# A fused retention and mixture-of-experts kernel: whole scores for the first eight tiles, earlier weights and tokens, and a new order of the first pass

## The chip, the cores and the metric

The kernel runs on one NeuronCore of a Trainium2 chip. The core has a matrix engine (TensorE; the profile calls its products PE and its weight loads PEld), VectorE (DVE), ScalarE (ACT), GpSimd (POOL) and SyncE (SP, which here only issues DMAs and reads registers). The metric is the device time of one execution in microseconds; lower is better.

## The reference, cut to what matters

The inputs are q, k, v (8 batches, 8 heads, 576 positions, 64 wide). Their retention output is the token matrix x (4608 x 512), and each token goes to one of 16 experts.

```
scores = q @ k.T / sqrt(64);  ret = scores * gamma[h] ** (i - j) for i >= j, else 0;  attn = ret @ v
x = attn, heads side by side                          # 4608 x 512
g = argmax(x @ w_group);  e = argmax(x @ w_expert[g]) # 4 groups of 4 experts
out[token] = g_w * e_w * (relu(x @ w1[g, e]) @ w2[g, e])   # 512 -> 1024 -> 512, g_w and e_w: softmax weights
```

## The kernel before

**Retention.** The tokens are cut into 36 tiles of 128 (t = 0 to 35; every ninth holds the last 64 positions of two batches). A loop over t works on several tiles at once. ACT scales the eight heads of v (`vs`, eight instructions, `scale(t + 1)`). TensorE multiplies the scaled values with the masked scores (`px`, `av(t - 1)`), adds to a running state (`pst`, `state(t)`), adds the part of the state (`px<-a,st`, `inter(t - 1)`) and makes the next scores (`pss`, `scores(t + 1)`). DVE scales the finished tile into `xT` (`turned(t - 1)`) and masks the new scores into `sT` (`masked(t + 1)`). There is one `px` buffer, so that the next `px` waits for `turned`. The scores leave out the blocks above the diagonal: 16 products of 64 x 64 weights and 128 or 64 columns per tile, on the four quarters of the array. Each f32 product leaves two PE records and two PEld records.

**Routing.** For each group of three tiles TensorE makes the logits (`plt`, then turned, `pl`), DVE picks the expert (`choose`: lg, mx, df, oh, ob), counts places (`pp`, `places`: pr, sl) and weighs (`weigh`: wt). TensorE turns each tile (`pxt`, `xnat_pe`), ACT writes it, weighted, to `xt` (`xnat_out`), and POOL writes token numbers beside it (iota) and scatters its rows into the DRAM buffer `xs`, sorted by expert (`xnat_store`).

**Experts.** 17 passes (p = 0 to 16) of eight steps f: `layer1(p, f)` makes `ph`, ACT takes relu to `hh`, `layer2(p, f)` adds to `py`. Weights come in four pieces a pass (`load_piece`, 2 x 512 KB, tiles `r`); they and the tokens are split into a high and a low part on ACT and DVE (`wh`, `wl`), except for the first six steps of pass 0 (`WHOLE`), which multiply in plain f32. Pass 0 handles the first 256 tokens of the fullest expert of the first tiles, which `pick(0)` finds while the retention still runs; `expert_of` reads its number into a register of SP, `xload(p)` loads the tokens (four DMAs, `xb<-xs`, for pass 0 256 rows of 2112 bytes), and `xturn` turns them on DVE. Pass 1 needs all tokens scattered. The last 128 columns of work (p = 16) end the kernel (`last1`: `phn`; `last_tr`: `pth`); one scatter of POOL each writes the results.

**Order.** After the set-up each engine runs its instructions in the order of the code (`Ordered`, `pin`), and all of them show as line L117, where the helper issues them. SP's loads, too, stay in the code's order: a load that waits holds up those behind it. The loads of tiles and of weights share two rings of seven buffers (`r1`, `r2`). The change touches the constants, `xnat_pe`, `xnat_out`, `xnat_store`, `layer1`, `scores`, the set-up loads, the retention loop from t = 31 (r = t - 26), the first two passes and the last.

Of the kernel before, what the change touches and what calls it, by code (L numbers as in the profile page):

```python
# [7 lines left out]
F32 = mybir.dt.float32  # L8
F32R = mybir.dt.float32r
# [19 lines left out]
WHOLE = 6  # L29
RB = 7  # L30
LOADS = 7
WARM = 32
NS = N + P
NT = N // P
NPIECE = 4
# [31 lines left out]
def moe_retention(ctx, tc, qk, kv, wgt, w1, w2, c_f, out):  # L67
# [92 lines left out]
    def load_piece(i):  # L160
        if i < len(pieces):
            raws[i] = wload(*pieces[i])
# [5 lines left out]
    def whole(p, f):  # L168

        return p == 0 and f < WHOLE  # L170
# [18 lines left out]
    def nblocks(p):  # L189
        return -(-CS[p] // 32)  # L190

    def natural(p):
        return p in (0, E)
# [136 lines left out]
    def xnat(t):  # L330
        xnat_pe(t)
        xnat_out(t)
        xnat_store(t)

    def xnat_pe(t):

        T = tiles[t]
        T["pxt"] = ps_tr.tile([P, NKC, P], F32, name=f"pxt_{t}", tag="tr")
        for i in range(NKC):
            pe.transpose(T["pxt"][:, i, :], T["xT"][:, i, :], ident)  # L340

    def xnat_out(t):
        T = tiles[t]
        g_ = tiles[T["grp"][-1]]
        r = t - T["grp"][0]
        pxt = T["pxt"]
        xt = T["xt"] = gp.tile([P, Q, WQ], F32, name=f"xt_{t}", tag="xt", bufs=3)
        act.activation(xt[:, :, 0:DQ], pxt, AF.Copy, scale=g_["wt"][:, r : r + 1])

    def xnat_store(t):  # L350
        T = tiles[t]
        g_ = tiles[T["grp"][-1]]
        r = t - T["grp"][0]
        xt = T["xt"]
        for b, s0, p0, n in T["rng"]:
            pool.iota(
                xt[p0 : p0 + n, :, DQ:WQ].bitcast(I32), pattern=[[1, Q], [0, WQ - DQ]],
                base=Q * (b * S + s0), channel_multiplier=Q,
            )
# [160 lines left out]
    def without():  # L520
        dve.tensor_scalar(mi0, sln, picked["c0"], float(BIG), ALU.is_ge, ALU.mult)

    obs = []
    wgp = gp.tile([P, NKC, 32], F32, name="wgp")


    with ExitStack() as ac:
# [70 lines left out]
        pw = ps_sm.tile([P, P], F32, name="pw", tag="sm")  # L598
# [26 lines left out]
        def scores(t):  # L625

            T = tiles[t]
            for i in range(0, NP, 2):  # L630
# [95 lines left out]
        for t in range(NT + 1):  # L726
# [60 lines left out]

# [60 lines left out]
    def layer1(p, f):  # L848
        i = p * NPIECE + f // 2
        C = CS[p]  # L850
        if (p, f) == (0, 0):
            ph = ps_st.tile([P, CMAX], F32, name=f"ph_{p}_{f}", tag="tr")
        elif p == 0:
            ph = psy.tile([P, CMAX], F32, name=f"ph_{p}_{f}", tag=f"py{f % 2}")
        else:
            pool_ = (ps_sm, ps_tr, ps_sm, ps_st)[f % 4]
            ph = pool_.tile([P, CMAX], F32, name=f"ph_{p}_{f}", tag="sm" if f % 2 == 0 else "tr")
        cs = slice((f % 2) * P, (f % 2) * P + P)
        hh = mp.tile([P, CMAX], F32R, name=f"hh_{p}_{f}", tag="hh", bufs=4)
        if whole(p, f):  # L860
            for kc in range(NKC):
                pe.matmul(
                    ph[:, :C], raws[i][0][:, kc, cs], xTf[p][:, kc, :C], start=kc == 0, stop=kc == NKC - 1
                )
            act.activation(hh[:, :C].bitcast(F32), ph[:, :C], AF.Relu)
            hts[p, f] = (hh.bitcast(F32), None)
            return
        wh, wl = wsp[i, 0]
        xh, xl = xTs[p]
        n = 0  # L870
        for kc in range(NKC):
            for a, b in ((wh, xh), (wh, xl), (wl, xh)):
                pe.matmul(
                    ph[:, :C], a[:, kc, cs], b[:, kc, :C], start=n == 0, stop=n == 3 * NKC - 1
                )
                n += 1
        C32 = 32 * nblocks(p)
        if f == 0 and C32 > C and not natural(p):

            dve.memset(hh[:, C:C32].bitcast(F32), 0.0)  # L880
        hl = mp.tile([P, CMAX], F32R, name=f"hl_{p}_{f}", tag="hl", bufs=4)
        act.activation(hh[:, :C], ph[:, :C], AF.Relu)
        dve.scalar_tensor_tensor(
            hl[:, :C], ph[:, :C], 0.0, hh[:, :C].bitcast(F32), ALU.max, ALU.subtract
        )
        hts[p, f] = (hh, hl)

    def layer2(p, f):
        if f == 0:
# [95 lines left out]
    for p in range(E):  # L985
        for f in range(NFC):
            pc = p * NPIECE + f // 2
            if p == 0:
                new = {2: (4, 5), 3: (6,), 5: (7,)}.get(f, ())
            else:  # L990
                new = range(pc + 3, pc + 5) if f % 2 == 0 else ()
            for i in new:
                if i not in raws and (i >= len(pieces) or pieces[i][0] in ereg):
                    load_piece(i)
            layer1(p, f)
            if (p, f) == (0, 0):
# [7 lines left out]
            if (p, f) == (0, 1):  # L1004
                expert_of(1)
                choose(NT - 1)
                xnat(NT - 4)
            if (p, f) == (0, 2):
                places_pe(NT - 1)
                places(NT - 1)  # L1010
                weigh(NT - 1)
                xnat(NT - 3)
# [13 lines left out]
            if prev is not None:  # L1026
                layer2(*prev)
                if f == 0:
                    for i in range(NKC if p > 1 else 2):
                        yturn(p - 1, i) if p > 1 else finish(0, i)  # L1030
            if (p, f) == (0, 2):
                tiles_counted()
                xnat(NT - 2)
                count_experts()
            if (p, f) in ((0, 4), (0, 5)):
                next(ranks, None)
            if (p, f) == (0, 6):
                expert_of(2)
            if (p, f) == (0, 7):
                next(ranks, None)  # L1040
# [6 lines left out]
            if f == (4 if p > 0 else 7) and p + 2 <= E:  # L1047
                xpad(p + 2)
            if f == (5 if p > 0 else 7):
                xload(p + 2)  # L1050
            if (p, f) == (2, NFC - 3):
                ov = overflow_places(cp)
# [9 lines left out]
            if f == NFC - 1 and p + 1 < E:  # L1062
                ids(p + 1)
            if (p, f) in ((5, NFC - 1), (10, NFC - 1), (14, NFC - 1), (E - 1, NFC - 2)):

# [301 lines left out]
```

## Time and profile before

| | |
|---|---|
| three timed runs | 604.39, 605.51, 606.35 us (median 605.51) |
| the profiled execution | 606.85 us, of which the span of its instructions is 605.1 us |
| PE busy | 584.0 us (97%), 6191 products |
| DVE, ACT, POOL busy | 430.2, 325.2, 263.3 us |
| retention | to about 149 us; pass 0 to about 182 us; then experts |

Durations below come from the one profiled execution. A row of a timeline is: start, duration, engine, line, operation, what it writes and reads, count, and in brackets how long the engine was idle before it and what ended that. PE ends are modelled, so the distance of two starts says more than a duration. "issue" is idle time for which the profile shows nothing to wait for.

### The profile page before, as it was taken

To read this page: it belongs to the slowest core of one execution; us is meant where nothing else is said; L and a number is where in the kernel's file an instruction comes from. 1 tells how busy PE (TensorE), PEld (TensorE's weight loads), DVE (VectorE), ACT (ScalarE), POOL (GpSimd) and SP (SyncE) were. 2 spreads that over 40 slices of the span, in tenths; PEclk is the share of its full clock that TensorE was granted. 3 is DMA by queue.
4 is the path that set the end of the run, shared out by engine and by line. 5 is a ranking of instruction groups with operands and counts; after the bars stand their busy time and mean duration, and the time that the engine had idled before them with its cause. 6 is when DMAs were issued, how large, how long until landed. Compare 5 with 4: busy or idle time off the path is not lost.

```text
span 605.1 us, 16614 instructions
## 1 busy us (share of the span) xinstructions
PE 584.0 (97%) x6191; PEld 549.7 (91%) x6191; DVE 430.2 (71%) x977; ACT 325.2 (54%) x849; POOL 263.3 (44%) x392
## 2 busy tenths in 40 slices
PE   7889999998999999999999999999999999999995
PEld 7778788777668999999999999999999999999994
DVE  3777677677477666997757675867768677686773
ACT  4677877865346434445435454544545455455553
POOL 0022322333313037494645537373563734636554
PEclk8999999999999999999999999999999999999999
DMA  8999999956983942819465563838467394674921
GB/s 332 416 384 341 344 344 337 353 183 194 381 261 97 349 199 77 298 40 340 111 265 146 230 235 145 284 115 311 130 245 249 123 334 118 259 240 153 369 93 35
DMA packets 62546, 143.11 MB, mean 237 GB/s; under 512 B 9313, under 2 KB 30185, under 8 KB 62464
## 3 DMA queue, kind: packets, MB, share of 16 engines
q1 hardware_dynamic: 53072, 121.59, 57.1%
q0 software_dynamic: 9248, 20.35, 9.4%
q8 instruction: 49, 0.80, 0.5%
q14 instruction: 33, 0.27, 0.1%
q10 hardware_dynamic: 144, 0.10, 0.1%
HBM read 121.67 MB, written 24.88 MB: 242 GB/s over the span
## 4 chain that ended last, share of the span: by engine, by line
PE 87%; DMA 5%; DVE 2%; issue 2%; POOL 1%; ACT 1%; SPq 0%; POOLq 0%; ACTq 0%; DVEq 0%
PE py L117 34%; PE ph L117 34%; PE px L117 7%; PE pss L117 4%; PE pxt L117 3%; PE pst L117 2%; DMA b<-in_kv 2%; PE plt L117 2%; POOL out L117 1%; DMA r<-in_w 1%; DMA xb<-xs 1%; DMA a<-in_qk 1%; PE pl L117 1%; DMA xs<-xt,sl 1%; PE phn L117 0%
## 5 line engine op out<-in xcount | busy, mean ns | idle before, releaser
L117 POOL DMA_INDIRECT out<-y,ii x152 | 167.2, 1100 | 51.0 <-issue 33.8
L117 DVE TENSOR_TENSOR wl<-r,wh 128x512 fp32r<-128x512 f32 x260 | 167.8, 687 | 8.3 <-ACT wh L117 4.5
L117 ACT ACTIVATE hh<-ph 128x356 fp32r<-128x356 f32 (+16 forms) x128 | 53.8, 420 | 212.6 <-PE ph L117 143.1
L117 PE MATMUL ph<-xTh_m,wh 128*128 128x356 f32 (+15 forms) x488 | 147.5, 302 | 0.8 <-ACT xTh_m L117 0.8
L117 ACT CAST wh<-r 128x512 fp32r<-128x512 f32 x260 | 146.9, 617 | 0.0
L117 PE MATMUL ph<-xTl_m,wh 128*128 128x356 f32 (+15 forms) x488 | 146.7, 301 | 0.1
L117 PE MATMUL ph<-xTh_m,wl 128*128 128x356 f32 (+15 forms) x488 | 146.6, 300 | 0.0
L117 PE MATMUL py<-hh,wh 128*128 128x288 f32 (+17 forms) x480 | 145.1, 302 | 0.0
L117 PE MATMUL py<-hl,wh 128*128 128x356 f32 (+14 forms) x480 | 144.7, 301 | 0.0
L117 PE MATMUL py<-hh,wl 128*128 128x356 f32 (+14 forms) x480 | 144.6, 301 | 0.0
L117 DVE SCALAR_TENSOR_TENSOR hl<-ph,hh 128x356 fp32r<-128x356 f32 (+15 forms) x122 | 56.7, 465 | 103.0 <-ACT hh L117 69.9
L117 POOL COPY pace<-hh 1x1 f32<-1x1 f32 x140 | 34.6, 247 | 140.4 <-ACT hh L117 138.4
L117 PEld LDWEIGHTS ph<-xTh_m,wh 128*128 128x128 f32 x488 | 92.0, 189 | 1.7 <-ACT xTh_m L117 1.2
L117 PEld LDWEIGHTS ph<-xTl_m,wh 128*128 128x128 f32 x488 | 92.0, 189 | 0.9 <-DVE xTl_m L117 0.4
L117 PEld LDWEIGHTS ph<-xTh_m,wl 128*128 128x128 f32 x488 | 92.2, 189 | 0.0
L117 PEld LDWEIGHTS py<-hh,wh 128*128 128x128 f32 x480 | 90.5, 189 | 0.2
L117 PEld LDWEIGHTS py<-hl,wh 128*128 128x128 f32 x480 | 90.4, 188 | 0.2 <-DVE hl L117 0.2
L117 PEld LDWEIGHTS py<-hh,wl 128*128 128x128 f32 x480 | 90.5, 189 | 0.0
L117 POOL DMA_INDIRECT xs<-xt,sl x36 | 35.9, 998 | 119.5 <-DVE ob L117 47.1
L117 ACT ACTIVATE vs<-b,cf 128x64 f32<-128x64 f32 x288 | 72.4, 335 | 7.9 <-DMA b<-in_kv 7.9
L117 DVE TENSOR_TENSOR sT<-pss,masks 128x512 f32<-128x512 f32 x72 | 46.0, 681 | 15.9 <-PE pss L117 10.7
L117 PE MATMUL px<-sT,vs 128*64 128x128 f32 x576 | 40.1, 280 | 2.2 <-DVE xT L117 1.7
(167 smaller groups left out, 615.8 us busy)
## 6 DMA issues: line engine op xcount, KB each, us to landing
r<-in_w SPq DMA_DIRECT2D x138, 512.0 KB
a<-in_qk SPq DMA_DIRECT2D x35, 512.0 KB
b<-in_kv SPq DMA_DIRECT2D x35, 512.0 KB
xb<-xs SPq DMA_DIRECT2D x24, 148.5 KB
xb<-xs SPq DMA_DIRECT2D x20, 165.0 KB
out<-y,ii POOLq DMA_INDIRECT x152
xb<-xs SPq DMA_DIRECT2D x12, 181.5 KB
xb<-xs SPq DMA_DIRECT2D x4, 198.0 KB
```

Of the source, the lines that this page charges most:

```text
L117: i_ = f(*a, **k)
```

## The change

The first eight tiles make their scores whole: eight products of 64 x 128 weights and 128 columns a tile, with the two head halves on the upper and the lower rows of the array. The 32 warming products of 128 columns become 8 of 512. The constants `gq` load after tile 1 instead of tile 0, and `wgp` and the rest of `cf` after tile 3 instead of tile 1. The token numbers (`xnat_rows`) are written before ACT fills `xt`. At the end of the retention the weight pieces load one tile earlier, the first two ahead of the tokens; the tokens of pass 0 are turned before tile 34 is finished on DVE, and the first product of pass 0 stands before the last tile's `px`. Pass 0 is reordered, parts of the ranking, the pads and the loads for pass 2 move into pass 1, and in the last pass each split of weights comes one place earlier.

```diff
-WARM = 32
+WARM = 8
+FULL = 8
...
+    def xnat_rows(t):
+        T = tiles[t]
+        xt = T["xt"] = gp.tile([P, Q, WQ], F32, name=f"xt_{t}", tag="xt", bufs=3)
+        for b, s0, p0, n in T["rng"]:
+            pool.iota(
...
     def xnat_out(t):
...
-        xt = T["xt"] = gp.tile([P, Q, WQ], F32, name=f"xt_{t}", tag="xt", bufs=3)
+        if "xt" not in T:
+            xnat_rows(t)
+        xt = T["xt"]
...
-            if t == 0:
+            if t == 1:
                 sp.dma_start(gqs[0], c_f[:, KC_GQ:KC_ALL].rearrange("p (x j) -> p x j", x=4))
-            if t == 1:
+            if t == 3:
                 sp.dma_start(wgp, wgt.rearrange("p (c e) -> p c e", c=NKC))
                 sp.dma_start(cf[:, KC_UP:KC], c_f[:, KC_UP:KC])
...
-            pe.matmul(pw, ones, ones, start=True, stop=True)
+            pe.matmul(pw, ones, ones.unsqueeze(1).to_broadcast([P, 4, P]), start=True, stop=True)
...
+            if t < FULL:
+                for i in range(NP):
+                    for o in range(2):
+                        r = slice(o * D, o * D + D)
+                        pe.matmul(
+                            pss[:, o, i * P : i * P + P], T["kT"][r, i, :], T["qT"][r, i, :],
+                            start=True, stop=True,
+                        )
+                return
...
+            if r == 9:
+                xturn(0, 0, 2)
+                xturn(0, 1, 2)
             if t + 1 < NT:
                 scale(t + 1)
...
-            if r in (6, 7, 8, 9):
+            if r in (5, 6, 7, 8):
+                load_piece(r - 5)
                 if r == 6:
                     xload(0)
-                load_piece(r - 6)
             if r == 9:
-                xturn(0, 0, 2)
-                xturn(0, 1, 2)
+                layer1(0, 0)
...
-            if (p, f) == (0, 0):
+            if (p, f) == (0, 1):
                 places_pe(NT - 4)
                 places(NT - 4)
                 logits(NT - 1)
                 xnat(NT - 6)
-                xnat(NT - 5)
-                gate_pe(NT - 1)
                 pick(1)
...
             if (p, f) == (0, 3):
-                xnat(NT - 1)
+                xnat(NT - 2)
+                xnat_rows(NT - 1)
+                count_experts()
+                xnat(NT - 1, ps_sm)
                 xload(1)
+                load_piece(6)
...
+            if (p, f) == (0, 1):
+                gate_pe(NT - 1)
+                choose(NT - 1)
+                xnat(NT - 5)
             if (p, f) == (0, 2):
+                xnat(NT - 3)
                 tiles_counted()
...
+            if (p, f) == (1, 2):
+                xpad(2)
+            if (p, f) == (1, 3):
+                xload(2)
...
         if pc == 0:
+            split(2 * E * NPIECE + 3)
             layer2(*prev)
         last1(pc)
...
         for k in range(2):
-            split(2 * (E * NPIECE + pc) + 3 + k)
+            split(2 * (E * NPIECE + pc) + 4 + k)
```

On SP, at the expert number of pass 0 (`e0i`; `xb` are the tokens, `r_0_0` the first weight piece), the order before is:

```order
L117 DMA b_2557<-in_kv 128x1024
L201 TENSOR_LOAD e0i
L201 ISA x2
L201 TENSOR_LOAD e0i
L201 ISA x2
L117 ISA
L117 DMA xb_2892<-xs 32x8x132
```

and in the changed kernel:

```order
L203 TENSOR_LOAD e0i
L203 ISA x2
L119 ISA
L119 DMA r_0_0_2724<-in_w 128x1024
L119 ISA
L119 DMA r_0_0_2725<-in_w 128x1024
L119 ISA
L119 DMA r_0_1_2808<-in_w 128x1024
L119 ISA
L119 DMA r_0_1_2809<-in_w 128x1024
L119 ISA
L119 DMA xb_2812<-xs 32x8x132
```

Two pieces of weights (four DMAs) now stand ahead of the tokens, and no longer behind them.

On PE, from the last `pl` of the retention loop (`ph_0` and `ph_1` are the first products of pass 0, `py` their second layer), the order before is:

```order
L117 MATMUL pl_3114<-cf,lt_3075 128x128 x3
L117 MATMUL px_3145<-sT_3060,vs_3006 64x128 x8
L117 MATMUL px_3145<-a_2537,st_2652 64x64 x8
L117 MATMUL px_3145<-a_2537,st_3032 64x64 x8
L117 MATMUL ph_0_3193<-xTf_3128,r_0_0_2899 128x256 x4
```

and in the changed kernel:

```order
L119 MATMUL pl_3036<-cf,lt_2993 128x128 x3
L119 MATMUL ph_0_3043<-xTf_3007,r_0_0_2724 128x256 x4
L119 MATMUL px_3064<-sT_2977,vs_2923 64x128 x8
L119 MATMUL px_3064<-a_2449,st_2564 64x64 x8
L119 MATMUL px_3064<-a_2449,st_2949 64x64 x8
L119 MATMUL ph_1_3112<-xTf_3007,r_0_0_2724 128x256 x4
```

The first product of pass 0 now stands between `pl` and the last tile's `px`, and the second follows that tile at once.

On DVE, where the last pass begins (`hl_7` belongs to the last step of pass 15, `wl_16_1` to the second piece of the last pass, `y` is the turned result of pass 15), the order before is:

```order
L117 SCALAR_TENSOR_TENSOR hl_7_9235<-ph_7_9221,hh_7_9222 128x260
L117 TENSOR_TENSOR wl_16_1_9239<-r_16_1_8991,wh_16_1_9238 128x512 x2
L117 STREAM_TRANSPOSE y_9283<-py_0_8967 128x9x32
L117 STREAM_TRANSPOSE y_9283<-py_1_8968 128x9x32
L117 STREAM_TRANSPOSE y_9283<-py_2_8969 128x9x32
L117 STREAM_TRANSPOSE y_9283<-py_3_8970 128x9x32
L117 TENSOR_TENSOR wl_16_1_9316<-r_16_1_8992,wh_16_1_9315 128x512 x2
```

and in the changed kernel:

```order
L119 SCALAR_TENSOR_TENSOR hl_7_9147<-ph_7_9133,hh_7_9134 128x260
L119 TENSOR_TENSOR wl_16_1_9151<-r_16_1_8903,wh_16_1_9150 128x512 x2
L119 TENSOR_TENSOR wl_16_1_9169<-r_16_1_8904,wh_16_1_9168 128x512 x2
L119 STREAM_TRANSPOSE y_9201<-py_0_8879 128x9x32
L119 STREAM_TRANSPOSE y_9201<-py_1_8880 128x9x32
```

Two `wl` instructions now stand ahead of the four transposes of `y`, after which POOL's last stores run.

## Rows read from the trace of the kernel before

**Rows 1.** The page: engines over the span, and PE over 40 slices

```profile
PE 584.0 (97%) x6191; PEld 549.7 (91%) x6191; DVE 430.2 (71%) x977; ACT 325.2 (54%) x849; POOL 263.3 (44%) x392
...
PE   7889999998999999999999999999999999999995
```

**Rows 2.** Timeline of ACT at the start: the scaled v of tile 2

```profile
13.59 2.02 ACT L117 ACTIVATE vs<-b,cf 128x64 f32<-128x64 f32 x8 [1.05 <-DMA b<-in_kv]
```

**Rows 3.** Timeline of PE, 0 to 40 us

```profile
15.91 0.69 PE L117 MATMUL pst<-vs,b 128*64 128x64 f32 x16 [0.79 <-ACT st L117]
...
17.01 0.85 PE L117 MATMUL pss<-a 64*64 64x128 f32 x32
18.01 1.09 PE L117 MATMUL px<-sT,vs 128*64 128x128 f32 x16
19.04 0.69 PE L117 MATMUL pst<-vs,b 128*64 128x64 f32 x16
...
30.69 0.85 PE L117 MATMUL pss<-a 64*64 64x128 f32 x32
31.46 0.66 PE L117 MATMUL pxt<-cf,xT 128*128 128x128 f32 x4
...
32.82 1.09 PE L117 MATMUL px<-sT,vs 128*64 128x128 f32 x16 [0.32 <-DVE xT L117]
```

**Rows 4.** Chain of waits, 0 to 60 us: two stretches without a reason

```profile
26.83 0.91 issue
...
34.02 0.62 issue
```

**Rows 5.** The page's DMA queues: the one that carries instructions

```profile
q8 instruction: 49, 0.80, 0.5%
```

**Rows 6.** Busy time by stretch: engines, granted clock, DMA share, GB/s

```profile
10.00:12.00 2.00, 2.00 (x44) 1.88 (x38) 0.70 (x2) 1.74 (x8) 0.00 (x0) 0.58 1.02 415
...
142.00:145.00 3.00, 3.00 (x64) 2.04 (x58) 2.46 (x8) 3.00 (x12) 1.18 (x2) 1.00 0.88 185
```

**Rows 7.** Timeline of PE, 128 to 192 us: waits around pass 0

```profile
147.61 1.09 PE L117 MATMUL px<-sT,vs 128*64 128x128 f32 x16 [0.70 <-DVE xT L117]
...
150.00 1.97 PE L117 MATMUL ph<-xTf,r 128*128 128x256 f32 x8 [0.67 <-DMA r<-in_w]
...
154.29 0.66 PE L117 MATMUL pxt<-cf,xT 128*128 128x128 f32 x4 [0.83 <-ACT xt L117]
...
181.77 0.43 PE L117 MATMUL ph<-xTh_m,wh 128*128 128x356 f32 x1 [0.76 <-ACT xTh_m L117]
```

**Rows 8.** Timeline of DVE at the end of the retention

```profile
146.87 0.69 DVE L117 TENSOR_TENSOR xT<-px,gq 128x512 f32<-128x512 f32 x1 [2.37 <-PE pxt L117]
147.47 1.29 DVE L117 STREAM_TRANSPOSE xTf<-xb 128x512 f32<-128x512 f32 x2
```

**Rows 9.** Timeline of SP: loads of pass 0

```profile
141.39 1.92 SPq L117 DMA_DIRECT2D xb<-xs  x4
...
144.49 17.83 SPq L117 DMA_DIRECT2D r<-in_w  x14
```

**Rows 10.** Timeline of POOL: the first of the last four scatters

```profile
164.35 0.99 POOL L117 DMA_INDIRECT xs<-xt,sl  x1 [3.27 <-ACT xt L117]
```

**Rows 11.** Chain of waits, 125 to 195 us: tokens of pass 1

```profile
168.89 3.90 DMA xs<-xt,sl
...
174.47 4.71 DMA xb<-xs
```

**Rows 12.** The page's costliest groups (busy us, mean ns of one | idle before): the splits on DVE

```profile
L117 DVE TENSOR_TENSOR wl<-r,wh 128x512 fp32r<-128x512 f32 x260 | 167.8, 687 | 8.3 <-ACT wh L117 4.5
```

**Rows 13.** Timeline of POOL at the end: first and last store

```profile
585.76 0.97 POOL L117 DMA_INDIRECT out<-y,ii  x1 [6.34 <-DVE y L117]
...
599.61 0.97 POOL L117 DMA_INDIRECT out<-y,ii  x1 [1.33 <-ACTq L1182]
```

**Rows 14.** Timeline of ACT at the end

```profile
598.75 0.58 ACT L117 COPY y<-py 128x512 f32<-128x512 f32 x1 [1.75 <-PE py L117]
```

More of the change, by code (lines that the diff above doesn't have):

```diff
@@ L328, in moe_retention, with xnat, xnat_pe @@
     ps_sm = ctx.enter_context(tc.tile_pool(name="ps_sm", bufs=2, space=PSUM))
-    def xnat(t):
-        xnat_pe(t)
+    def xnat(t, pool_=None):
+        xnat_pe(t, pool_)
         xnat_out(t)
         xnat_store(t)
-    def xnat_pe(t):
+    def xnat_pe(t, pool_=None):
         T = tiles[t]
-        T["pxt"] = ps_tr.tile([P, NKC, P], F32, name=f"pxt_{t}", tag="tr")
+        T["pxt"] = (pool_ or ps_tr).tile(
+            [P, NKC, P], F32, name=f"pxt_{t}", tag="sm" if pool_ else "tr"
+        )
         for i in range(NKC):
             pe.transpose(T["pxt"][:, i, :], T["xT"][:, i, :], ident)
+    def xnat_rows(t):
[3 more added lines that the diff above has]
+            pool.iota(
+                xt[p0 : p0 + n, :, DQ:WQ].bitcast(I32), pattern=[[1, Q], [0, WQ - DQ]],
+                base=Q * (b * S + s0), channel_multiplier=Q,
+            )
     def xnat_out(t):
@@ L354, in xnat_store @@
         xt = T["xt"]
[L355 to L359, printed above, removed]
         apart("xs", pool.indirect_dma_start(
@@ L521, in without, with layer1 @@
         dve.tensor_scalar(mi0, sln, picked["c0"], float(BIG), ALU.is_ge, ALU.mult)
+    def layer1(p, f):
+        i = p * NPIECE + f // 2
+        C = CS[p]
+        if (p, f) in ((0, 0), (0, 1)):
+            ph = ps_st.tile([P, CMAX], F32, name=f"ph_{p}_{f}", tag="tr")
+        elif p == 0:
+            ph = psy.tile([P, CMAX], F32, name=f"ph_{p}_{f}", tag=f"py{f % 2}")
+        else:
+            pool_ = (ps_sm, ps_tr, ps_sm, ps_st)[f % 4]
+            ph = pool_.tile([P, CMAX], F32, name=f"ph_{p}_{f}", tag="sm" if f % 2 == 0 else "tr")
+        cs = slice((f % 2) * P, (f % 2) * P + P)
+        if (p, f) == (0, 0):
+            hh = wp.tile([P, NKC, EARLY], F32, name="hh_0_0", tag="wl0", bufs=3)[:, 0]
+        else:
+            hh = mp.tile([P, CMAX], F32R, name=f"hh_{p}_{f}", tag="hh", bufs=4)
+        if whole(p, f):
+            for kc in range(NKC):
+                pe.matmul(
+                    ph[:, :C], raws[i][0][:, kc, cs], xTf[p][:, kc, :C], start=kc == 0, stop=kc == NKC - 1
+                )
+            hf = hh if f == 0 else hh.bitcast(F32)
+            act.activation(hf[:, :C], ph[:, :C], AF.Relu)
+            hts[p, f] = (hf, None)
+            return
+        wh, wl = wsp[i, 0]
+        xh, xl = xTs[p]
+        n = 0
+        for kc in range(NKC):
+            for a, b in ((wh, xh), (wh, xl), (wl, xh)):
+                pe.matmul(
+                    ph[:, :C], a[:, kc, cs], b[:, kc, :C], start=n == 0, stop=n == 3 * NKC - 1
+                )
+                n += 1
+        C32 = 32 * nblocks(p)
+        if f == 0 and C32 > C and not natural(p):
+            dve.memset(hh[:, C:C32].bitcast(F32), 0.0)
+        hl = mp.tile([P, CMAX], F32R, name=f"hl_{p}_{f}", tag="hl", bufs=4)
+        act.activation(hh[:, :C], ph[:, :C], AF.Relu)
+        dve.scalar_tensor_tensor(
+            hl[:, :C], ph[:, :C], 0.0, hh[:, :C].bitcast(F32), ALU.max, ALU.subtract
+        )
+        hts[p, f] = (hh, hl)
     obs = []
@@ L590, in moe_retention @@
             loads(t, "b")
-            if t == 0:
+            if t == 1:
                 sp.dma_start(gqs[0], c_f[:, KC_GQ:KC_ALL].rearrange("p (x j) -> p x j", x=4))
-            if t == 1:
+            if t == 3:
                 sp.dma_start(wgp, wgt.rearrange("p (c e) -> p c e", c=NKC))
                 sp.dma_start(cf[:, KC_UP:KC], c_f[:, KC_UP:KC])
-        pw = ps_sm.tile([P, P], F32, name="pw", tag="sm")
+        pw = ps_sm.tile([P, 4, P], F32, name="pw", tag="sm")
         for i in range(WARM):
-            pe.matmul(pw, ones, ones, start=True, stop=True)
+            pe.matmul(pw, ones, ones.unsqueeze(1).to_broadcast([P, 4, P]), start=True, stop=True)
         def late_consts(t):
@@ L629, in scores @@
             T = tiles[t]
+            if t < FULL:
+                for i in range(NP):
+                    for o in range(2):
+                        r = slice(o * D, o * D + D)
+                        pe.matmul(
+                            pss[:, o, i * P : i * P + P], T["kT"][r, i, :], T["qT"][r, i, :],
+                            start=True, stop=True,
+                        )
+                return
             for i in range(0, NP, 2):
@@ L845, in rank_experts @@
         dve.tensor_scalar(mil, el, cr[:, 0:1], float(BIG), ALU.is_ge, ALU.mult)
-    def layer1(p, f):
-        i = p * NPIECE + f // 2
-        C = CS[p]
-        if (p, f) == (0, 0):
[L852 to L886, printed above, removed]
     def layer2(p, f):
@@ L988, in moe_retention @@
             if p == 0:
-                new = {2: (4, 5), 3: (6,), 5: (7,)}.get(f, ())
+                new = {2: (4, 5), 5: (7,)}.get(f, ())
             else:
@@ L994, in moe_retention @@
                     load_piece(i)
+            if (p, f) == (0, 0):
+                prev = (p, f)
+                continue
+            ahead = (p, f) == (0, WHOLE)
+            if ahead:
+                layer2(*prev)
             layer1(p, f)
-            if (p, f) == (0, 0):
+            if (p, f) == (0, 1):
                 places_pe(NT - 4)
@@ L1000, in moe_retention @@
                 xnat(NT - 6)
-                xnat(NT - 5)
-                gate_pe(NT - 1)
                 pick(1)
-            if (p, f) == (0, 1):
                 expert_of(1)
-                choose(NT - 1)
+            if (p, f) == (0, 2):
                 xnat(NT - 4)
-            if (p, f) == (0, 2):
                 places_pe(NT - 1)
@@ L1025, in moe_retention @@
                 split(2 * pc + f % 2 + 3)
-            if prev is not None:
+            if not ahead:
                 layer2(*prev)
-                if f == 0:
-                    for i in range(NKC if p > 1 else 2):
-                        yturn(p - 1, i) if p > 1 else finish(0, i)
+            if f == 0:
+                for i in range(NKC if p > 1 else 2):
+                    yturn(p - 1, i) if p > 1 else finish(0, i)
+            if (p, f) == (0, 1):
+                gate_pe(NT - 1)
+                choose(NT - 1)
+                xnat(NT - 5)
             if (p, f) == (0, 2):
+                xnat(NT - 3)
                 tiles_counted()
-                xnat(NT - 2)
-                count_experts()
-            if (p, f) in ((0, 4), (0, 5)):
+            if (p, f) in ((0, 4), (1, 0), (1, 1)):
                 next(ranks, None)
@@ L1038, in moe_retention @@
                 expert_of(2)
-            if (p, f) == (0, 7):
-                next(ranks, None)
+            if (p, f) == (1, 1):
+                ids(1)
             if p > 1 and f > 0:
@@ L1046, in moe_retention @@
                     ystore(p - 1, b)
-            if f == (4 if p > 0 else 7) and p + 2 <= E:
+            if (p, f) == (1, 2):
+                xpad(2)
+            if (p, f) == (1, 3):
+                xload(2)
+            if f == 4 and p and p + 2 <= E:
                 xpad(p + 2)
-            if f == (5 if p > 0 else 7):
+            if f == 5 and p:
                 xload(p + 2)
@@ L1061, in moe_retention @@
                     xsplit(p + 1, kc)
-            if f == NFC - 1 and p + 1 < E:
+            if f == NFC - 1 and 0 < p < E - 1:
                 ids(p + 1)
```

1 line of the change is left out of this document (removed).

## The prediction

> **What bounds the kernel now.** I read the page first. TensorE is busy 97% of the span, and in the 40 slices its digit is 9 from about 190 us to 580 us [rows 1]. The diff touches nothing there that TensorE executes, so a gain can come only from places where TensorE is not full: the start (the first slices show 7 and 8), the end of the retention with pass 0, and the last microseconds. Then I read the timelines of PE, DVE, ACT, POOL and SP in those places, and the chain of waits for what the last link is. The start holds one wait for ACT, 0.79 us, in a chain that ends at a load [rows 2, 3], and two stretches of 0.91 and 0.62 us for which no reason is shown [rows 4]. Around pass 0 TensorE waits four times, 0.70, 0.67, 0.83 and 0.76 us [rows 7]. Here 0.3% (1.8 us) is what a measurement can tell from no change, so all the visible waits together, about 5.3 us, are only three times that bound.
>
> The sum is made against the profiled execution: 606.85 us, of which 605.1 is the span and 1.75 lies around it. The median of the three runs is 605.51, and I shift the result by that difference.
>
> **1. Constants behind the tiles: -0.5 (0 to -0.8).** Loads run at their limit at the start: DMA share 1.02 and 415 GB/s between 10 and 12 us [rows 6], so 512 KB take 1.26 us, and what is queued earlier is paid by all behind it. In the changed order about 320 KB (`wgp` and the rest of `cf`) go from before tile 2 to behind tile 3, and `gq` (256 KB) only from tile 0 to tile 1, still ahead. So `b` of tile 2 lands 0.79 us earlier (320/512 x 1.26), its `vs`, which waited 1.05 us for it, starts at about 12.8 instead of 13.59 [rows 2], and the 0.79 us that `pst` waits behind them at 15.91 [rows 3] become small. For tiles 4 and 5 nothing changes, since all constants lie ahead of them in either order. TensorE does not get all of it, since the whole scores make it later itself: I keep 0.5.
>
> **2. Stretches without a reason: -1.53 (0 to -1.53).** 6191 products have as many weight loads, so 12382 instructions of PE came in; 49 instruction transfers of 0.80 MB are listed [rows 1, 5], about 253 instructions to a block if all are PE's. The two stretches lie 7.19 us apart [rows 4], about one block of the retention's instructions, while the DMA share is at its limit. I read them as TensorE waiting for its next block of instructions behind the tokens' loads. Each of the 16 f32 products of a tile's scores leaves two records (x32 [rows 3]) and two weight loads, 64 instructions; eight whole ones leave 32. The warming takes 8 products and 8 loads instead of 32 and 32. By tile 8 that is 8 x 32 + 48 = 304 fewer, more than one block, so a block lasts longer and its successor has time to come in. The other bound is that the stalls only move. I take the whole 1.53.
>
> The Trainium skill ("Runtime: NRT & Kernel Launch", section "Instruction fetch mechanics") says that instructions are refilled in blocks of 256 and that crossing a block costs little and is mostly hidden. Our transfer size agrees; the stretches of 0.91 and 0.62 us speak against "hidden". By the page this term would be 0 and the time 604.6; it is a rival below on the same ground of rows.
>
> **3. Whole scores: +0.7 (+0.2 to +1.25, and far more if no two run together).** A score took 0.77 us from start to start when work follows at once (30.69 to 31.46 [rows 3]). The whole one is 8 products of 128 columns in pairs on upper and lower rows; `px` has just this number of f32 columns in its 8 products over the two column halves, 18.01 to 19.04, that is 1.03 us [rows 3]. So +0.25 a tile. The bound above is no pair side by side: four products of 128 columns on the full array take 0.66 (`pxt` at 31.46 [rows 3]), 0.165 for each of its 4, and with two head halves 16 x 0.165 = 2.64 if each of the 16 records costs as much, +1.87. Below: the 0.85 that the present scores are busy, +0.1. I take `px`, the nearest in form. At tiles 3 and 4, `px` starts 1.00 us after the scores (17.01 to 18.01 [rows 3]), because it waits for DVE to scale the tile before; there a score of 1.02 costs 0.1 with DVE's share. At tiles 5 and 6 other products follow and it costs all 0.25; at tile 7 `px` waits 0.32 for DVE [rows 3], which hides it. 0.1 x 2 + 0.25 x 2 = 0.7. If that cover were gone, five tiles would cost 1.25. The warming has the same columns in fewer products, and TensorE first waits for tokens anyway: 0, if the granted clock, 0.58 between 10 and 12 us [rows 6], falls at the same time.
>
> The Trainium skill ("TensorEngine Tiling (Array Packing)", section "Key Properties") says that a change of tiling mode drains TensorE. Before, the state's part and the scores share 64 x 64; now the scores have a mode of their own. The rows show no such price: `pxt` on the full array starts 0.77 us after the scores before it, inside their modelled 0.85 [rows 3]. [...]
>
> **4. End of the retention and pass 0: -1.4 (+0.55 to -3.0).** Before, the weights' pieces issue at 144.49, behind the tokens from 141.39, which wait for scatters [rows 9]; now two pieces stand ahead, right behind the expert number, where DMA had room. The tokens may then be delayed by what is left of 2 MB, but 185 GB/s over 142 to 145 us are 0.556 MB [rows 6], which is pass 0's tokens (256 x 2112 bytes = 0.541 MB): they were in by about 145, and their transposes started at 147.47 without a wait [rows 8]. Now the transposes (1.29 us) come first on DVE, into the 2.37 us in which DVE waited for `pxt` before 146.87 [rows 8], so `xT` of tile 34 stays where it was. The first product of pass 0 fills the 0.70 us before the last `px` (1.97 us of work), `px` starts at 148.85 instead of 147.61 and the second product at 150.57; before, the first product ended at 151.97. That is 0.70 + 0.67 = 1.4. The wait of 0.83 for `xt` [rows 7] goes in part, since `pxt` of the last tiles come one after another. POOL's last four scatters begin at 164.35, after 3.27 us idle for `xt` [rows 10]; `xt` is 1.4 earlier, and the token numbers are written before. So the last scatter (168.89), its landing (3.90), the load of pass 1's tokens (174.47, 4.71) [rows 11] and the product at 181.77 [rows 7] all move by 1.4 to 1.6. Without its four waits TensorE could start that product at 181.77 - 2.96 = 178.8, so the chain through POOL and DMA still decides, and 0.76 of wait can stay. Bounds: all four waits, -3.0; the token transposes 1.9 us late, +0.55. The loads of pass 2's tokens and parts of the ranking move into pass 1; their tokens are turned only at its fifth step, several microseconds after they can land, under full TensorE work: 0. `load_piece(6)` behind `xload(1)` no longer stands ahead of it on SP's queue: in favour, uncounted.
>
> **5. Tail: +0.3 (-0.7 to +0.6).** DVE makes two `wl` (167.8/260 = 0.645 each [rows 12], 1.29) ahead of the transposes of `y`. POOL's first store waits for these (585.76, 6.34 idle), and its ten stores follow at a distance of 0.3 us; the last at 599.61 idles 1.33 for ACT's `y` [rows 13, 14], 599.33 at its end. 1.29 later, the ninth store ends at 599.57 and the last can go at 599.9: +0.3. The split products are earlier by one place, so ACT's `y` may come 0.7 earlier; it then doesn't decide.
>
> **Sum.** -0.5 - 1.53 + 0.7 - 1.4 + 0.3 = -2.43; 606.85 - 2.43 = 604.42 for a profiled run, 605.51 - 2.43 = 603.1 for the median; I say 603.0.
>
> **Rivals.**
> A. The stretches without a reason are not the fetch of instructions, or only move. For: nothing names them. Against: their distance. Then term 2 is 0: 605.51 - 0.9 = 604.6, no measurable change. 0.22.
> B. The head halves do not run side by side. Then a whole score is 2.64 us and six tiles (2 to 7) pay 1.87 each, 11.2, less the 0.8 hidden under DVE (0.15 x 2, 0.25 and the start's 0.2): +10.4; with the other terms (-3.13) the time is 612.8, slower. It turns the sum from 1.42 us a score (0.77 + (3.13 + 0.8)/6) and can be measured from 1.72 (1.8 us more). For: no row shows two products of 64 rows and 128 columns together. Against: the present scores run four quarters together, 16 products in 0.77 us. 0.08.
> C. The weights ahead of the tokens delay them. A load of 512 KB takes 1.26 us; if all four loads are still ahead at 141.39 [rows 9], the tokens land at 145.4 + 4 x 1.26 = 150.4, the transposes (1.29) hold DVE's queue and with it `xT` of tile 34 and the last `px`, which starts at about 152.2. That is 4.6 later than 147.61, of which the first product (1.97) and its old wait (0.67) come back: +2.0 instead of -1.4, and the sum is +0.97, 606.5, no measurable change. For: DMA share 0.88 even now [rows 6]. Against: the pieces issue some 6 us earlier. 0.07.
> D. All four waits and both stretches go, and the tail gains: -0.8 - 1.53 + 0.3 - 3.0 = -5.0, 600.5. 0.07.
> Forecast: 0.56, with its own range 601.4 to 604.6.
>
> Faster by over 0.3% (below 603.7): 0.49 of the forecast, D, 0.01 of A, 0.57. Within: the forecast's rest 0.07, A 0.21, C 0.06, 0.34. Slower (above 607.3): B and 0.01 of C, 0.09. The range 600.6 to 605.8 leaves out B, most of C and half of D, under 0.2.
>
> **What would show it.** Right: `vs` of tile 2 at about 12.8; `pss` of the first tiles in 16 records over 1.0 us; no stretch without reason near 27 and 34 us; the first `ph` in front of the last `px` without a wait, and the second at about 149.2 (150.57 less the 1.33 that the start gains); the product of pass 1 that stood at 181.77 at about 179; the ninth store ending after ACT's last `y`. Wrong: `pss` of 1.4 us or more (B), the same idle stretches at another place (A), a wait of the token transposes for DMA (C), or the clock at half for longer than between 8 and 12 us.

## The result and the profile after

The changed kernel takes 613.9 us (median; 613.65 to 614.17) against 605.93 us for the kernel before beside it: ratio 1.0132, 95% interval 1.0105 to 1.0159. I forecast 603.0, with a range of 600.6 to 605.8. The span of the profiled execution went from 605.1 to 611.9 us, +6.8.

The page, TensorE's lines (engines over the span; PE and the granted clock in 40 slices):

```profile
PE 587.6 (96%) x6039; PEld 550.2 (90%) x6039; DVE 431.0 (70%) x977; ACT 325.8 (53%) x849; POOL 262.9 (43%) x392
...
PE   8999999996997999999999999999999999999995
...
PEclk9999999997998999999999999999999999999998
```

Slices 10 and 13, about 138 to 153 and 184 to 199 us, now hold a 6 and a 7, with clocks of 7 and 8; before, they held an 8 and a 9 [rows 1], and the clock was 9 in every slice after the first. The start is better than before, as these rows of PE show (a whole score and what follows, a later `px`, then three stretches without a reason):

```profile
12.17 1.16 PE L119 MATMUL pss<-a 64*128 64x128 f32 x16
13.26 1.09 PE L119 MATMUL px<-sT,vs 128*64 128x128 f32 x16
14.69 0.69 PE L119 MATMUL pst<-vs,b 128*64 128x64 f32 x16 [0.33 <-ACT st L119]
...
31.63 1.09 PE L119 MATMUL px<-sT,vs 128*64 128x128 f32 x16
...
45.26 0.33 PE L119 MATMUL pst<-vs,b 128*64 128x64 f32 x3 [1.15 <-issue]
...
51.23 0.21 PE L119 MATMUL pss<-a 64*64 64x64 f32 x1 [0.68 <-issue]
...
86.00 0.55 PE L119 MATMUL pss<-a 64*64 64x128 f32 x13 [0.99 <-issue]
```

The `px` that stood at 32.82 [rows 3] is at 31.63, 1.19 us earlier; a whole score costs 1.09 from start to start; the wait of 0.79 for ACT is 0.33. The stretches of [rows 4] are gone, and others stand further back, the three longest at 45, 51 and 86 us.

Then PE from the `px` of tile 34 to pass 1. In the kernel before, the first and the last of these rows were:

```profile
144.31 1.09 PE L117 MATMUL px<-sT,vs 128*64 128x128 f32 x16
...
186.22 0.32 PE L117 MATMUL ph<-xTh_m,wh 128*128 128x356 f32 x1
```

and after:

```profile
141.34 1.09 PE L119 MATMUL px<-sT,vs 128*64 128x128 f32 x16
...
148.55 3.78 PE L119 MATMUL ph<-xTf,r 128*128 128x256 f32 x8 [4.60 <-DVE xTf L119]
152.26 1.60 PE L119 MATMUL px<-sT,vs 128*64 128x128 f32 x16
...
187.24 0.47 PE L119 MATMUL ph<-xTh_m,wh 128*128 128x356 f32 x1 [4.53 <-ACT xTh_m L119]
...
192.48 0.33 PE L119 MATMUL ph<-xTh_m,wh 128*128 128x356 f32 x1
```

These rows hold most of the loss. At tile 34 the changed kernel is 2.97 us ahead. Then PE waits 4.60 us for the turned tokens, where it waited 0.70 [rows 7]. Behind that wait the product that took 1.97 [rows 7] takes 3.78 at a lowered clock, and the `px` after it 1.60 instead of 1.09. At the first product of pass 1 PE is ready at 187.24 - 4.53 = 182.71 (before 181.77 - 0.76 = 181.01, so already 1.70 late) and waits 4.53 where it waited 0.76: +5.47. The clock falls again, and the next step of pass 1 comes 6.26 us late: 186.22 before, 192.48 after. The tail brings the rest. The clock by stretch (engines, then granted clock, DMA share, GB/s; a value such as 0.83 is the mean of a stretch that lies partly at 1.00 and partly at 0.50, the lower of the two levels, 1.2 GHz):

```profile
140.00:150.00 10.00, 5.40 (x59) 3.75 (x56) 4.24 (x10) 2.87 (x9) 3.34 (x5) 0.83 0.88 251
150.00:160.00 10.00, 10.00 (x88) 6.86 (x87) 4.32 (x22) 2.07 (x5) 0.55 (x1) 0.83 0.27 108
...
180.00:190.00 10.00, 5.38 (x26) 4.50 (x25) 5.98 (x12) 3.62 (x9) 0.00 (x0) 0.87 1.06 339
```

The chain of waits, 125 to 210 us, SP's loads of weights ahead of it, and POOL in pass 0, name what each wait is for:

```profile
134.33 6.58 DMA xs<-xt,sl
141.01 0.34 SPq L119
...
142.63 4.44 DMA xb<-xs
...
175.59 2.78 DMA xs<-xt,sl
...
180.16 4.41 DMA xb<-xs
```

```profile
132.20 2.10 SPq L119 DMA_DIRECT2D r<-in_w  x4
```

```profile
162.66 0.99 POOL L119 DMA_INDIRECT xs<-xt,sl  x1 [2.02 <-ACT hh L119]
...
171.19 0.15 POOL L119 IOTA xt<- 128x16 int32 x1 [3.54 <-DMA xs<-xt,sl]
...
175.59 1.01 POOL L119 DMA_INDIRECT xs<-xt,sl  x1 [0.30 <-issue]
```

In the kernel before, POOL issued the scatter that the tokens wait for at 137.90, and its one wait for an `xt` buffer in pass 0 was 0.63 us:

```profile
137.90 0.99 POOL L117 DMA_INDIRECT xs<-xt,sl  x1 [2.00 <-ACT xt L117]
...
160.94 0.15 POOL L117 IOTA xt<- 128x16 int32 x1 [0.63 <-DMA xs<-xt,sl]
```

The tokens of pass 0 wait for one scatter that takes 6.58 us to land, with two pieces of weights (2 MB) issued just ahead of it; before, the tokens followed their scatter after 3.49 us (137.90 to 141.39). So they are issued at 141.01, hardly earlier than the 141.39 of [rows 9], though tile 34 is 2.97 us earlier. They are turned from 147.19 on, before from 147.47 [rows 8]: in time for the kernel before, which still had tile 35 to do, and too late for this one, whose order has the first product of pass 0 ahead of tile 35. And in pass 0 the iota of tile 34 waits at 171.19: there are three `xt` buffers, and the one it needs is still read by the scatter issued at 162.66. ACT's `xt`, the last scatter (175.59 instead of 168.89 [rows 11]) and pass 1's tokens stand behind it.

The tail (POOL's first and last two stores, ACT's last `y`):

```profile
593.49 1.48 POOL L119 DMA_INDIRECT out<-y,ii  x1 [7.91 <-DVE y L119]
...
605.16 0.97 POOL L119 DMA_INDIRECT out<-y,ii  x1 [0.30 <-issue]
606.44 0.97 POOL L119 DMA_INDIRECT out<-y,ii  x1 [0.30 <-issue]
```

```profile
605.12 0.58 ACT L119 COPY y<-py 128x512 f32<-128x512 f32 x1 [1.75 <-PE py L119]
```

The first store waits 7.91 instead of 6.34 [rows 13], and the last stands behind POOL's own stores instead of behind ACT's `y` [rows 14].

### The profile page after: what moved, and what is told of

It reads as the page before. It is cut to its first block, busy times and chain, and to the rows that moved or that the text cites. A ratio compares the mean times of both kernels' runs of the same rounds, so it can differ in the third digit from the quotient of the medians.

```text
span 611.9 us, 16308 instructions
## 1 busy us (share of the span) xinstructions
PE 587.6 (96%) x6039; PEld 550.2 (90%) x6039; DVE 431.0 (70%) x977; ACT 325.8 (53%) x849; POOL 262.9 (43%) x392
## 4 chain that ended last, share of the span: by engine, by line
PE 85%; DMA 5%; DVE 3%; issue 2%; POOL 1%; ACT 1%; SPq 1%; POOLq 0%; DVEq 0%; ACTq 0%
PE ph L119 35%; PE py L119 34%; PE px L119 6%; PE pss L119 3%; PE pxt L119 3%; PE pst L119 2%; DMA xs<-xt,sl 2%; DMA b<-in_kv 1%; DMA xb<-xs 1%; PE plt L119 1%; DMA gq<-c_f 1%; POOL out L119 1%; SPq L119 1%; PE phn L119 1%; ACT vs L119 1%
```

## The experiments

Theory 1: the weights ahead hold up the scatter and with it the tokens. Theory 2: the tokens' place ahead of tile 34 on DVE costs. Theory 3: the new order of pass 0 costs. Each ratio is to the kernel before on the same chip, with its 95% interval. All edits of the first group are to the changed kernel.

**e1: weights behind the tokens again.**

```diff
-            if r in (5, 6, 7, 8):
-                load_piece(r - 5)
+            if r in (6, 7, 8, 9):
                 if r == 6:
                     xload(0)
+                load_piece(r - 6)
```

> The changed kernel with one part undone: at the end of the retention the weight pieces are loaded as in the kernel before (the tokens of pass 0 first, each piece one tile later); the place of the token transposes and of the first product stays changed. Theory 1 (the 2 MB of weights ahead hold up the scatter on which the tokens wait: 134.33 to 140.9 us, 6.58 instead of about 3.4): the tokens issue at about 138, their transposes start at about 144 instead of 147.2, the 4.60 us wait of PE goes to under 1.5 or is split with a wait for the weights, the granted clock stays 1.00 between 140 and 160 us, and the time is about 608 (606.5 to 610). Theory 2 (the place of the transposes ahead of the scaling of tile 34 on DVE is what costs, whatever the loads do): PE still waits over 3 us there, time 612 to 614. Theory 3 (the reordered pass 0 costs: xt buffers that wait for scatters to land): the wait of 4.53 us before the first product of pass 1 stays, and the time stays over 611.

**e2: one piece ahead** (`xload(0)` ahead of `load_piece(r - 5)` at r = 6).

> The changed kernel with one piece of weights (1 MB, two loads) ahead of the tokens of pass 0 instead of two. Theory 1 (bytes ahead of the scatter): half the dose, the tokens issue at about 138 to 139.5 instead of 141.0, time between that of the changed kernel and that with no piece ahead, about 609 to 611. Theory 2 (place on DVE): no change, 613 to 614. Theory 3 (pass 0): no change.

**e3: the transposes behind tile 34's scaling again** (the two `xturn` move from ahead of `scale` to ahead of `layer1(0, 0)`).

> The changed kernel with one part undone: the token transposes stand behind the scaling of tile 34 on DVE again; the weights stay ahead of the tokens and the first product ahead of the last px on PE. Theory 1: the tokens still land at about 147, the first product still waits for them and holds the last px behind it, so PE still waits over 3.5 us; time 612 to 614. Theory 2: the wait of 4.60 us goes below 1.5, time 608 to 610. Theory 3: 612 to 614.

**e4: the whole end of the retention as before** (e1 and e3, and `layer1(0, 0)` at r = 10).

> The changed kernel with the whole end of the retention as before: loads of weights behind the tokens, transposes behind the scaling of tile 34, the first product of pass 0 behind the last px; start, pass 0 after it, pass 1 and tail stay changed. Theory 1 or 2: the start's 1.85 us and little else is left, 604 to 607. Theory 3 (the new order of pass 0 itself costs): the first product of pass 1 still waits 2 us or more for the tokens of pass 1, 608 to 611.

Measured: e1 609.54 us, 1.0055 (1.0018 to 1.0092); e2 608.31, 1.0034 (1.0009 to 1.0059); e3 617.24, 1.016 (1.0118 to 1.0202); e4 608.05, 1.0048 (1.0013 to 1.0083). SP's loads of pass 0's tokens in e4, e2 and e3:

```profile
136.57 2.78 SPq L119 DMA_DIRECT2D xb<-xs  x4
```

```profile
137.07 1.91 SPq L119 DMA_DIRECT2D xb<-xs  x4
```

```profile
142.97 1.89 SPq L119 DMA_DIRECT2D xb<-xs  x4
```

The scatter that each waits for was issued at 133.60, 132.95 and 135.61. From that issue to the tokens' issue it takes 2.97 us with no piece ahead (e1: 132.90 to 135.88, 2.98; the kernel before 3.49), 4.12 with one, 6.68 (changed kernel) and 7.36 (e3) with two. The dose is clear in the scatter's delay, and theory 1 stands; in the times only two pieces stand out, since e1 and e2 cannot be told apart (e2 was expected at 609 to 611). In e1, e2 and e4 PE waits 1.5, 0.5 and 0 us there, and the clock stays at 1.00 from 140 to 160 us. Theory 2 alone falls: with the new places kept and the loads back (e1) the wait is 1.5 us, and undoing the place on DVE alone (e3) made it no better, since the first product on PE still waits (6.2 us). No run put both the transposes and the first product back with two pieces ahead, so how much of the wait the new places add to the late tokens is not shown. But some 5 us (1.0132 to 1.0048) are not enough: e4, with nothing of the end changed, is still slower than the kernel before, as theory 3 has it. POOL in e4:

```profile
164.03 0.15 POOL L119 IOTA xt<- 128x16 int32 x1 [3.53 <-DMA xs<-xt,sl]
165.54 0.99 POOL L119 DMA_INDIRECT xs<-xt,sl  x1 [1.35 <-ACT xt L119]
...
168.54 0.97 POOL L119 DMA_INDIRECT xs<-xt,sl  x1 [0.30 <-issue]
```

PE starts pass 0 at 144.80 there, 5.2 us before the 150.00 of [rows 7], and yet the last scatter is at 168.54, as good as the old 168.89; the lead is lost at the iota, and PE waits 4.3 us before pass 1.

**e5: e4 with own memory for the last two `xt`** (unused memory of the split weights).

```diff
+        if t >= NT - 2:
+            own = wp.tile(..., tag="wh0" or "wh1", bufs=3)
+            xt = T["xt"] = own.rearrange("p k e -> p (k e)")[:, 0 : Q * WQ].rearrange(...)
```

> The kernel of the run before (end of the retention as in the kernel before, all else as changed), and the xt tiles of the last two token tiles get memory of their own, so that POOL's iota and ACT's xt no longer wait for a buffer of three that an earlier scatter still reads. Theory 3a (the buffer is what holds the new order of pass 0: iota at 164.03 waits 3.53 us for the scatter of three tiles before): that wait is gone, the last scatter goes at about 165 instead of 168.5, the tokens of pass 1 are issued at about 168 instead of 171.5, PE's wait of 4.3 us before the first product of pass 1 falls to about 1, the clock stays at 1.00 in 180 to 190 us, and the time is about 604 (603 to 605.5) against 608.05. Theory 3b (the scatters land late whatever buffer is used, since weights fill the DMA queues): the wait moves to the tokens' load, PE still waits 2.5 us or more, 606.5 to 608. Theory 3c (the tail or the start costs, not pass 0): no change in time.

**e11: e4 with the first weights of pass 1 behind its tokens.**

```diff
-                new = {2: (4, 5), 5: (7,)}.get(f, ())
+                new = {4: (4, 5, 6), 5: (7,)}.get(f, ())
...
                 xload(1)
-                load_piece(6)
```

> The kernel with the end of the retention as before and all else as changed, but the first three weight pieces of pass 1 (six loads, 3 MB) are loaded behind the tokens of pass 1 instead of two of them ahead. Theory 3b (weights in the DMA queues hold up the scatters of pass 0, which land after about 8 us): the scatters at about 155 to 160 land in under 4.5 us, the iota's 3.53 us wait goes below 0.5 although the buffers are the same, and the last scatter goes at about 165; the weights come later, so that a wait for them may stand before pass 1: 604 to 608. Theory 3a (the buffers alone, landing time not raised by the weights): the wait stays at 3 us or more, 608 to 611.

Measured: e5 602.82 us, 0.9926 (0.9897 to 0.9956); e11 607.44, 1.0012 (0.9991 to 1.0034). In e5 the iota's wait is gone, the last scatter goes at 167.20 and PE waits 2.1 us before pass 1, instead of 4.3; the clock from 180 to 190 us is 0.83 as in e4, not 1.00 as expected. That is more gain (1.2% of ratio, over 7 us) than the 2.2 us less of wait account for; the profiled execution (606.17) lies 3.4 us above the median, so its rows tell little of the excess, which stays open. In e11 the same buffers no longer make the iota wait, the last scatter goes at 165.41, and what comes next is the weights:

```profile
170.80 5.13 DMA r<-in_w
175.95 0.63 ACT wh L119
```

So the third buffer and the late landing act together: in e4 the scatter issued at 155.51 frees its buffer only for the iota at 164.03, 8.5 us later, with weights in the queues. More buffers or fewer weights ahead take the wait away; the first costs only memory that was free, the second makes the weights late (PE waits 2.9 us for `hh`, at a clock of 0.84 and 0.65 from 170 to 190 us).

**e12: one piece ahead and own `xt`** (e2 and e5's edit in the changed kernel), and **e13: two pieces ahead and own `xt`**.

> The changed kernel with two repairs: one weight piece ahead of the tokens of pass 0 instead of two, and memory of their own for the xt tiles of the last two token tiles. If the two causes are what the runs so far show (scatters held up by weights in the DMA queues, and the xt buffers), PE waits less than 1 us before the first product of pass 0 and less than 2.5 us before the first of pass 1, the retention and pass 0 end some 4 us earlier than in the changed kernel, and the ratio to the kernel before is 0.991 (0.987 to 0.995), as good as or better than with the end of the retention as before (0.9926). If either cause is a story, the ratio stays near 1.003, that of the kernel with one piece ahead alone.

> The changed kernel, two pieces of weights ahead of the tokens as it has them, with memory of their own for the xt tiles of the last two token tiles. If the two causes are separate, the wait of 4.60 us before the first product of pass 0 stays and the granted clock falls behind it, and the wait of 4.53 us before the first product of pass 1 falls below 2.5 us: 613.9 less about 4, ratio 1.006 (1.003 to 1.009). If the second wait only follows from the first (everything late is late together), no change: 1.012.

Measured: e12 602.5 us, 0.9925 (0.9902 to 0.9949); e13 610.37, 1.0075 (1.0047 to 1.0103). PE's waits before passes 0 and 1 in e13 and then in e12 (us in total, times, longest):

```profile
PE ph L119 <- DVE xTf L119: 6.4, 1, 6.4
...
PE ph L119 <- ACT xTh_m L119: 1.1, 1, 1.1
```

```profile
PE ph L119 <- ACT xTh_m L119: 1.3, 1, 1.3
...
PE ph L119 <- DVE xTf L119: 0.3, 1, 0.3
```

In e13 the second wait fell from 4.53 to 1.1 though the first stayed (6.4): two causes, and they come apart. In e12 both are small, and the clock is 1.00 from 140 to 200 us. Taking away the buffer wait is worth 0.6% (1.0132 to 1.0075), taking away one of the two pieces then 1.5%. e12 beats the kernel before and the changed one; it ties with e5.

**e14: e2 with the old order of passes 0 and 1** (the loop over passes of the kernel before, without its `layer1(0, 0)`).

> The changed kernel with one piece of weights ahead of the tokens instead of two and the order of pass 0 and pass 1 as in the kernel before; start, place of the token transposes and of the first product, and tail as changed. If the new order of pass 0 gains nothing in itself, the ratio is the 0.9925 of the kernel with the new order and its own xt memory, or better (0.990 to 0.994); if the new order is worth 1 us or more once it does not wait, 0.994 to 0.997.

Measured: 604.26 us, 0.9968 (0.9942 to 0.9994). The new order seems worth some 0.4% once its `xt` doesn't wait, though the intervals of e14 and e12 touch.

**e6 to e10: parts on the kernel before.** e6 is the whole start, e8 `FULL = 8` alone, e9 the warming alone, e10 the constants alone; e7 is e6 with the tail's splits. Their diffs are the lines of the change on these parts.

> The kernel before with the changed start alone: whole scores in eight tiles, eight warming products of 512 columns, the constants two tiles later. By the two profiles the products of tile 9 come 1.85 us earlier, so the time is about 604.2 against 606 (ratio 0.997, 0.995 to 0.999). Rival: the stretches without a reason have only moved to later tiles, then no change (0.999 to 1.001).

> The kernel before with the changed start and the changed tail (each split of weights in the last pass one place earlier), end of the retention and pass 0 as before. If the tail's change costs what the profile shows (POOL's stores back to back to the end, +0.5 us), the ratio to the kernel with the changed start alone is 1.001 (0.9995 to 1.002); if the earlier splits shorten PE's last waits, 0.998 to 1.000.

> The kernel before with whole scores in the first eight tiles and nothing else. Theory of blocks (fewer instructions, stretches without a reason go from the first 40 us): no such stretch before 40 us, +0.3 us a tile for the scores of 1.09 instead of 0.77 us; ratio 0.998 (0.996 to 1.000). On the clock: if the longer scores at 4.6 us are what kept the granted clock at 1.00 from 8 to 12 us in the changed kernel, it is 1.00 here; if it was the warming, it is about 0.57 as before.

> The kernel before with 8 warming products of 512 columns instead of 32 of 128, nothing else. The same columns, PE busy to 4.65 us in both: no change in time (0.999 to 1.001) and a clock of about 0.57 from 8 to 12 us, unless it was the warming that kept the clock; then 1.00 there and 0.998.

> The kernel before with the constants loaded two tiles later (gq after tile 1, wgp and the rest of cf after tile 3), nothing else. vs of tile 2 starts about 0.8 us earlier (12.8 instead of 13.59), PE's wait of 0.79 us at 15.91 gets smaller by 0.5; ratio 0.999 (0.998 to 1.000). The stretches without a reason stay where they were.

| | median us | ratio | 95% interval |
|---|---|---|---|
| e6 start | 603.67 | 0.9962 | 0.9941 to 0.9983 |
| e7 start and tail | 602.77 | 0.9943 | 0.9920 to 0.9967 |
| e8 whole scores | 605.7 | 0.9985 | 0.9955 to 1.0015 |
| e9 warming | 606.15 | 0.9994 | 0.9974 to 1.0014 |
| e10 constants | 606.06 | 0.9993 | 0.9973 to 1.0014 |

By its ratio the start gains 2.3 us (0.9962) as a whole; no part of it alone can be told from no change. The tail costs nothing that can be measured. In e10 `vs` of tile 2 started at 12.33 (12.8 expected), but the wait of `pst` for ACT behind it was still 0.72 us (14.66), not 0.5 less than 0.79; with the whole scores (e6) it was 0.34. Of the clock, PE and the windows in e8 and then in e9:

```profile
7.38 2.15 PE L118 MATMUL pst<-vs,b 128*64 128x64 f32 x16 [1.49 <-ACT vs L118]
...
8.00:10.00 2.00, 2.00 (x16) 1.83 (x17) 0.00 (x0) 1.00 (x5) 0.00 (x0) 0.50 1.05 395
```

```profile
6.57 2.00 PE L117 MATMUL pst<-vs,b 128*64 128x64 f32 x16 [0.39 <-ACT vs L117]
...
16.52 1.07 PE L117 MATMUL pst<-vs,b 128*64 128x64 f32 x16 [2.23 <-ACT st L117]
...
8.00:10.00 2.00, 2.00 (x50) 1.82 (x50) 0.53 (x1) 0.76 (x4) 0.00 (x0) 1.00 1.04 399
...
14.00:20.00 6.00, 3.77 (x72) 3.29 (x70) 1.93 (x4) 5.39 (x22) 0.00 (x0) 0.72 1.03 421
```

Nothing here says that the scores or the warming set it, though a single execution each cannot rule it out. The clock fell to its lower level where PE had just stood still for a load (1.49 us in e8, 2.23 in e9), and not after 0.39 or, at 11.75, 1.34 in e9. Length alone does not decide, since in e1 the clock stayed at 1.00 behind the wait of 1.50 us before pass 0. When the first loads land differs between executions: `vs` of tile 0 started at 7.18 before and at 6.17 in e9, which has the same loads.

## Why the prediction was wrong

- **Step 4 (-1.4) failed, twice.** I wrote that the tokens "may then be delayed by what is left of 2 MB" and set that against DMA room at 142 to 145 us. But the row that decides stands before it: the tokens wait for a scatter [rows 9], and it was this scatter that the weights held up, from 3.49 us to 6.68. Rival C named the cause at a wrong place and price: +2.0 instead of -1.4, that is 3.4 us, and only 0.07 of chance. Measured, the way from tile 34's `px` to the first product of pass 1 lost 2.97 + 5.47 = 8.4 us, and 0.8 more at the low clock behind it. With both causes repaired (e12) the change gains 0.75% (0.51 to 0.98), more than the 0.4% of the sum.
- **The second half of it I did not see at all.** I took "`xt` is 1.4 earlier" for granted. The new order puts four scatters of pass 0 within 7.2 us (159.45 to 166.65; before 9.3, 155.01 to 164.35) while eight loads of weights (4 MB, issued from 144.02) fill the queues; with three buffers the fifth tile waits for the second's scatter, 8.5 us after its issue. An `xt` is free only when its scatter has landed. The trace of the kernel before had the sign: the buffer of the scatter at 155.01 came free 5.93 us later, for the iota at 160.94 that waited 0.63. I priced a landing at the 3.90 us of [rows 11], which fell while the last weights drained (DMA share 1.06 from 169 to 170 us, 0.03 from 172 to 173).
- **The clock added to both.** A wait on PE was priced at its own length. Behind the first wait the product cost 1.8 us more (3.78 - 1.97) and the next `px` 0.5 (1.60 - 1.09); behind the second it was 0.8 us.
- **Step 1 was right as to ACT:** `vs` of tile 2 came at 12.37 (12.8 forecast) and PE's wait fell to 0.33. With the constants alone (e10) the wait stayed at 0.72, and no gain can be told from none.
- **Step 2 read the stretches rightly and priced them wrongly:** they left the first 40 us and came back later, the second half of rival A; up to the last pass they add up to 3.9 us before and 3.7 after. Rival A's first half, that it is not the fetch of instructions, is not borne out by the DMA records of the traces. Transfers of 16 KB on the instruction queue (q8, [rows 5]) ended at 26.50 and 33.04, and the two stretches of [rows 4] ended at 27.74 and 34.64. Of 84 such stretches of 0.15 us and more between 10 and 580 us in all 16 traces, 80 end 1.2 to 1.75 us after the end of such a transfer, where a moment taken at random does so in about one case of eleven. That the tokens' loads are what makes a block late is not shown.
- **Step 3 was right in kind:** 1.09 us a score (1.03 forecast), so rival B is refuted. The net cost of 0.7 us was not resolved (e8: 0.9955 to 1.0015).
- **Step 5 was right in its order:** the last store now stands behind POOL and starts 1.32 us after ACT's last `y` instead of 0.86, so 0.5 us (0.3 forecast); e7 against e6 shows no cost.
- The start's sum, -1.33 by steps 1 to 3, was measured as -2.3 (e6), within its interval. That is partly luck: its largest term, -1.53, did not come about, since the two stretches at 45 and 51 us stand in e6 as well (1.15 and 0.68 us). What gave the 2.3 us is open.
- In the working, the sum of rival D has four terms for five steps: with the bounds of steps 3 and 5 (+0.2 and -0.7) it would be -5.8. Nothing else hangs on it.

## What to carry to other kernels

A load moved ahead into idle DMA time is not free: look at which short transfers (scatters, gathers) run in that time, who waits for their landing, and how long they take with the queue full. When an order is tightened, count the buffers against the landing time, not against the compute time. A wait on TensorE can cost more than its length: here the clock was lower behind the waits of 2.1 to 6.4 us before passes 0 and 1, and not behind those of 1.1 to 1.5 us (e13, e12, e1).

## What the runs showed that was not expected

PE's stretches without a reason, which by the transfers above look like waits for instructions, differ much between the profiled executions: 0.2 us in all in that of e8, 1.9 in e6, 6.5 in e10. The profiled executions with little of it lie under their kernel's median (e8 -2.44 us, e6 -2.94), those with much above (e10 +2.71, e5 with 5.2 +3.35); over the 16 kernels the correlation is 0.79. So they go with much of the spread of about 3 us to either side, though a correlation does not show that they make it.

Two of them belong to the kernel: in all twelve kernels with the whole changed start a stretch stands at 44.5 to 45.8 us (1.15 us in ten of them) and one at 50.5 to 51.5. The later ones come and go while that code is the same: one of 1.4 to 2.0 us near 64 us stands in e2, e5, e12 and e14 and in none of the other eight. A later stretch that is seen in a single trace is thus no cost that a change can be credited with removing.
